# Fused attention and gated FFN: output weights loaded ahead of later pairs, wider weight rows, one value product later, a fifth E buffer

## The chip, the cores and the metric

The kernel runs on one core of a Trainium2 chip. The metric is the device time of one execution in microseconds (us); 3 to 12 executions of each kernel were taken, and medians are given.

## The reference, cut to what matters

```python
# attention: batch 8, 12 heads, 448 tokens, head size 64
scores = scale * q @ k.T;  attn = softmax(scores);  x = attn @ v      # -> 3584 tokens x 768
# FFN, width 1536
g = x @ w_gate;  val = x @ w_val
out = (g * sigmoid(g) * val) @ w_out                                  # float32
```

All inputs are float32; the kernel's DMAs cast them to float16 as they load.

## The kernel before

Two heads make a pair; 48 pairs are worked through in a loop. Step `pr` computes the scores and exponentials of pair `pr`, prepares a pair two or three steps ahead, takes products with v for two older pairs, and fills TensorE (PE) with FFN work of earlier tokens. PE, ScalarE (ACT), VectorE (DVE) and GpSimd (POOL) each do their instructions in the order of the program; the timelines below show it. GpSimd issues every casting load, so the order of loads is GpSimd's order of instructions. Parts that the argument touches:

```python
ep   = tc.tile_pool(name="ep", bufs=4)                      # E: exponentials of a pair
ps_a = tc.tile_pool(name="ps_a", bufs=1, space=PSUM)        # value products: one buffer
ps_f = tc.tile_pool(name="ps_f", bufs=3, space=PSUM)        # sums, transposes, FFN
WB = DF // 4                                                # gate and value weights: 4 tiles of 384 columns
def pv(p0, t, pool=None):      # value product of pairs p0, p0+1, half t: 16 matmuls
    acc = (pool or ps_a).tile(...)
    ...
def scaled(p0, t, acc):        # its eviction: VectorE multiplies by 1/sum, into the FFN's input X
    nc.vector.tensor_tensor(X[kk][...], acc[:, 0:S], R[p0][:], ALU.mult)
def prep(pr):                  # pairs 11 and up: POOL copies q, k; then a DMA transpose makes qkT
    ...
wq = {0: [("qk", 6), ("g", 0), ("v", 0)],
      1: [("V", 2), ("qk", 8), ("g", 1), ("v", 1)],
      3: [("g", 2), ("v", 2)],
      4: [("qk", 10), ("g", 3), ("v", 3)],
      5: [("V", 3)], 6: [("o", 0)], 7: [("o", 1)], 8: [("o", 2)]}      # loads by step
for pr in range(END):
    if not odd and 12 <= pr + LA < NPAIR:      # LA = 6
        load_qk16(pr + LA)                     # q and k of pairs pr+6, pr+7
    ... qk_half(pr, 0) ... prep(pr + 3) ...
    # even pr below 6: the sums of pairs pr-2, pr-1, copied and inverted (4 reciprocals) by VectorE
    # odd pr: scaled(pr - 3, 0, pv(pr - 3, 0)), loads of wq[pr], FFN work, qk_half(pr, 1)
    if work:
        scaled(pr - 3, 1, pv(pr - 3, 1))       # second half of the value product
```

Each third of the output weight (`wo`, 768 KB as float16) is one load. The first output product needs all three. FFN block 0 starts in step 6, once the attention of its tokens is done.

The softmax here doesn't subtract the row's maximum and nothing guards it: scores larger than these inputs give would overflow.

## Time and profile before

| | before |
|---|---|
| time, first rounds | 470.74 us median (469.92 to 472.1) |
| profiled span | 469.6 us |
| PE idle before 30.5, 67.2 to 72.0, after 464 | 4.9, 4.8, 4.4 us |
| first FFN matmul | 30.5 us |
| third 2 of the output weight lands / PE wants it | 72.0 / 67.2 us |
| PE clock halved | 70.2 to 77.0 us |

The page's chain of work that ended last, by engine, and its row of granted PE clock in 40 slices of 11.7 us (tenths of full speed):

```profile
PE 83%; DMA 13%; POOL 2%; issue 1%; ACT 0%; DVE 0%; ACTq 0%; POOLq 0%
PEclk9999997999999999999999999999999999999999
```

13% of the chain is DMA, yet 4.8 us is all that PE waits for a load: the chain was followed back from that one wait through the queue of loads to the start. Read it as "the end hangs on the queue until 72 us, and on PE after". The seventh slice has the slow clock.

### The profile page before, as it was taken

What the parts mean: (1) busy time and instruction counts of PE and PEld (TensorE: products, weight loads), DVE (VectorE), ACT (ScalarE), POOL (GpSimd) and SP (SyncE); (2) the same over time, 40 slices, a digit from 0 to 9 for tenths busy, and PEclk for the clock granted to TensorE, in tenths of its full rate; (3) what the DMA queues carried; (4) which work ended last, traced back from release to release, by engine and by line L of the source; (5) the groups of instructions that cost most, each with busy time, mean ns of one, the idle gap of its engine ahead of it and who ended that gap; (6) DMA issues with size and microseconds to landing.
All of it is one profiled execution on the core that took longest, in us unless ns stands there. A gap on an engine that the chain in (4) does not pass through costs nothing.

```text
span 469.6 us, 14109 instructions
## 1 busy us (share of the span) xinstructions
PE 455.5 (97%) x6357; PEld 228.0 (49%) x6357; DVE 237.8 (51%) x372; ACT 241.0 (51%) x348; POOL 105.3 (22%) x166
## 2 busy tenths in 40 slices
PE   7899978999999999999999999999999999999996
PEld 2344433444445555444445555444445556544453
DVE  2665662367764554546546535555456456334310
ACT  5986643765656546555446655455545552222221
POOL 8655624330450040310331131210200000000000
PEclk9999997999999999999999999999999999999999
DMA  9999999995864392944919566813423111100123
GB/s 135 195 201 200 203 170 201 151 151 60 109 93 68 36 130 60 144 77 39 140 23 126 95 96 104 116 29 75 73 33 54 36 36 35 36 6 30 35 67 101
DMA packets 80380, 44.23 MB, mean 94 GB/s; under 512 B 36672, under 2 KB 76864, under 8 KB 80320
## 3 DMA queue, kind: packets, MB, share of 16 engines
q0 software_dynamic: 40864, 23.37, 37.1%
q1 hardware_dynamic: 39392, 19.92, 23.9%
q8 instruction: 49, 0.80, 0.7%
q14 instruction: 11, 0.09, 0.1%
q10 hardware_dynamic: 64, 0.05, 0.0%
HBM read 47.19 MB, written 11.01 MB: 124 GB/s over the span
## 4 chain that ended last, share of the span: by engine, by line
PE 83%; DMA 13%; POOL 2%; issue 1%; ACT 0%; DVE 0%; ACTq 0%; POOLq 0%
PE gp L248 14%; PE op L245 13%; PE vp L248 12%; PE op L248 10%; PE vp L245 9%; PE s L182 8%; PE acc L196 7%; PE gp L245 6%; DMA wv<-in_moe_w_val_dram 5%; DMA wo<-in_moe_w_out_dram 5%; PE acc L218 3%; DMA wg<-in_moe_w_gate_dram 2%; DMA vt<-in_v_dram 1%; POOL k L118 0%; POOL q L118 0%
## 5 line engine op out<-in xcount | busy, mean ns | idle before, releaser
L189 ACT ACTIVATE E<-s 112x896 f16<-112x896 f32 x192 | 164.5, 916 | 29.1 <-PE s L182 29.1
L264 ACT ACTIVATE sg<-gp 128x384 f32<-128x384 f32 (+1 forms) x96 | 52.3, 544 | 85.8 <-PE gp L248 54.8
L276 DVE SCALAR_TENSOR_TENSOR t<-sg,gp 128x384 f32<-128x384 f32 (+1 forms) x96 | 58.6, 610 | 64.3 <-ACT sg L264 64.2
L307 ACT ACTIVATE osb<-op 128x384 f32<-128x384 f32 x55 | 27.0, 490 | 106.7 <-PE op L245 62.4
L248 PE MATMUL gp<-X,wg 128*32 128x512 f16 (+1 forms) x1416 | 78.1, 355 | 0.0
L245 PE MATMUL op<-wo,hts 128*128 128x384 f16 x396 | 69.9, 330 | 4.8 <-DMA wo<-in_moe_w_out_dram 4.8
L233 DVE RECIPROCAL R<-ssb 128x112 f32<-128x112 f32 x92 | 72.9, 827 | 0.7
L279 DVE SCALAR_TENSOR_TENSOR hts<-t,vp 128x384 f16<-128x384 f32 (+1 forms) x96 | 59.6, 621 | 22.9 <-PE vp L248 7.9
L248 PE MATMUL vp<-X,wv 128*32 128x512 f16 (+1 forms) x1224 | 66.9, 353 | 0.0
L210 DVE TENSOR_TENSOR X<-acc,R 128x448 f16<-128x448 f32 x48 | 29.9, 624 | 72.5 <-PE acc L196 70.9
L182 PE MATMUL s<-qkT 64*128 64x448 f16 x384 | 55.1, 357 | 3.6 <-ACT E L189 3.1
L245 PE MATMUL vp<-X,wv 128*128 128x384 f16 (+1 forms) x270 | 58.5, 353 | 0.0
L245 PEld LDWEIGHTS <-hts 128*128 128x128 f16 x396 | 38.4, 99 | 34.8 <-issue 9.2
L248 PEld LDWEIGHTS <-wg 128*32 128x32 f16 x1416 | 37.9, 97 | 29.5
L248 PE MATMUL op<-wo,hts 128*32 128x384 f16 x1104 | 48.9, 326 | 0.0
L127 POOL DMA_DIRECT2D vt<-in_v_dram x17 | 13.1, 768 | 155.6 <-PE acc L196 154.0
L245 PE MATMUL gp<-X,wg 128*128 128x384 f16 (+1 forms) x222 | 47.4, 350 | 0.0
L196 PE MATMUL acc<-E,vt 112*32 112x448 f16 x768 | 45.7, 360 | 0.1
L248 PEld LDWEIGHTS <-wv 128*32 128x32 f16 x1224 | 32.8, 97 | 25.4
L245 PEld LDWEIGHTS <-wv 128*128 128x128 f16 x270 | 25.3, 98 | 26.9 <-issue 4.8
L248 PEld LDWEIGHTS <-hts 128*32 128x32 f16 x1104 | 29.6, 97 | 16.3
L152 POOL COPY qk<-q 112x512 f16<-112x512 f16 x37 | 22.9, 619 | 56.2 <-DMA qkT<-qk 46.9
(37 smaller groups left out, 201.9 us busy)
## 6 DMA issues: line engine op xcount, KB each, us to landing
vt<-in_v_dram POOLq DMA_DIRECT2D x15, 336.0 KB, 5.0
q<-in_q_dram POOLq DMA_DIRECT2D x22, 224.0 KB, 5.8
k<-in_k_dram POOLq DMA_DIRECT2D x22, 224.0 KB, 7.1
out_dram<-osb SPq DMA_DIRECT2D x7, 336.0 KB, 3.1
wg<-in_moe_w_gate_dram POOLq DMA_DIRECT2D x8, 288.0 KB, 11.1
wv<-in_moe_w_val_dram POOLq DMA_DIRECT2D x8, 288.0 KB, 11.2
wo<-in_moe_w_out_dram POOLq DMA_DIRECT2D x3, 768.0 KB, 17.2
out_dram<-osb SPq DMA_DIRECT2D x8, 288.0 KB, 3.0
```

What stands on the lines that cost most here:

```text
L152: eng.tensor_copy(qk16[:, 1 - t].rearrange("p c h d -> p h c d"), src)
L182: nc.tensor.matmul(s[:, hx, 0:S], lhsT=t[ts(hx, 64)].rearrange("p c q -> p (c q)")[:, c * P : c * P + 128], rhs=t[ts(hx, 64), NC:, :].rear ...
L189: nc.scalar.activation(E[pr][:, c], s[0:P, :, 0:S], AF.Exp, scale=sm_scale)
L196: nc.tensor.matmul(acc[ts(j, 32), 0:S], lhsT=v16[g][:, 2 * r + j % 2, c, :].rearrange("p (d t) -> p t d", t=2)[:, t], rhs=E[p0 + j // 2][: ...
L210: nc.vector.tensor_tensor(X[kk][:, hp + t, ts(bb, S)], acc[:, 0:S], R[p0][:], ALU.mult)
L233: lambda i=i: nc.vector.reciprocal(rt[:, ts(i, P)], ssb[:, ts(i, P)]) for i in range(4)
L245: nc.tensor.matmul(dst, lhsT=lhsT, rhs=rhs, start=start, stop=stop)
L248: nc.tensor.matmul(dst[ts(j, 32), :], lhsT=lhsT[:, ts(j, 32)], rhs=rhs, start=start, stop=stop)
L264: nc.scalar.activation(sg[:, 0:n], gp[:, 0:n], AF.Tanh, scale=0.5)
L276: nc.vector.scalar_tensor_tensor(t1[:, 0:n], sg[:, 0:n], 1.0, gp[:, 0:n], ALU.add, ALU.mult)
L279: nc.vector.scalar_tensor_tensor(hts[:, fb, 0:n], t1[:, 0:n], 0.5 * HS, vp[:, 0:n], ALU.mult, ALU.mult)
L307: nc.scalar.activation(osb[:, ts(oh, OH)], op[:, 0:OH], AF.Copy, scale=1.0 / HS)
```

## The change

Intent: get the output weight in before PE wants it. (1) The last third goes ahead of q and k of pairs 14 and 15. (2) The last two quarters of the gate and value columns become one tile, so read rows are 3072 instead of 1536 bytes and there are four loads fewer; loads before them change places. (3) The second value product of pairs 0 and 1 moves from step 3 to step 4, which makes pair 0's E live longer, hence (4) five E buffers. (5) Both value products of step 6 go to the three-buffer pool.

```diff
-    ep = ... bufs=4
+    ep = ... bufs=5
-    WB = DF // 4                                   # four tiles of 384 columns
+    WSPL = [(0, 384), (384, 384), (768, 768)]      # three tiles
 wq:
-            1: [("V", 2), ("qk", 8), ("g", 1), ("v", 1)],
-            3: [("g", 2), ("v", 2)],
-            4: [("qk", 10), ("g", 3), ("v", 3)],
-            5: [("V", 3)],
-            6: [("o", 0)],
-            7: [("o", 1)],
-            8: [("o", 2)],
+            1: [("qk", 8), ("g", 1), ("v", 1)],
+            3: [("qk", 10), ("V", 2), ("g", 2), ("v", 2)],
+            4: [("qk", 12)],
+            6: [("V", 3), ("o", 0)],
+            7: [("o", 1), ("o", 2)],
-            if not odd and 12 <= pr + LA < NPAIR:
+            if not odd and 14 <= pr + LA < NPAIR:
-                halves = [pv(pr - 2, 0), pv(pr - 2, 1, ps_f)]
+                halves = [pv(pr - 2, t, ps_f) for t in range(2)]
-            if work:
+            if pr == 4:
+                scaled(0, 1, pv(0, 1))
+            if work and pr != 3:
                 scaled(pr - 3, 1, pv(pr - 3, 1))
```

More of the change, by code (lines that the diff above doesn't have):

```diff
@@ L70 @@
     attp = ctx.enter_context(tc.tile_pool(name="attp", bufs=4))
-    ep = ctx.enter_context(tc.tile_pool(name="ep", bufs=4))
+    ep = ctx.enter_context(tc.tile_pool(name="ep", bufs=5))
     xp = ctx.enter_context(tc.tile_pool(name="xp", bufs=2))
@@ L81 @@
     ident = consts.tile([P, P], FP16, name="ident")
-    WB = DF // 4
+    WSPL = [(0, 384), (384, 384), (768, 768)]
     wgv = {}
     for kind in "gv":
-        for i in range(4):
-            wgv[kind, i] = consts.tile([128, NCB, WB], FP16, name=f"w{kind}{i}")
+        for i, (m0, m) in enumerate(WSPL):
+            wgv[kind, i] = consts.tile([128, NCB, m], FP16, name=f"w{kind}{i}")
     def wslice(kind, fb, cb):
-        i, off = divmod(fb * 128, WB)
-        return wgv[kind, i][:, cb, ds(off, 128)]
+        i = min(fb // 3, 2)
+        return wgv[kind, i][:, cb, ds(fb * 128 - WSPL[i][0], 128)]
     wo = [consts.tile([128, NFB // 3, DM], FP16, name=f"wo{i}") for i in range(3)]
@@ L137, in load_w @@
         else:
-            src = (moe_w_gate if kind == "g" else moe_w_val)[:, ts(i, WB)].rearrange(
+            src = (moe_w_gate if kind == "g" else moe_w_val)[:, ds(*WSPL[i])].rearrange(
                 "(a p t) m -> t p a m", p=128, t=2
```

## The prediction

> **What bounds the kernel now.** I read the page first: TensorE (PE) is busy 97% of a 469.6 us span, so only its 14 idle us and any slow clock can be won without removing work, and the change removes none. The cut into stretches tells where those us are. Its columns are PE, weight load, VectorE, ScalarE and GpSimd busy us (instructions), granted PE clock, DMA share, GB/s.
>
> ```profile
> 0.00:30.50 30.50, 25.61 (x337) 11.10 (x337) 16.68 (x29) 23.33 (x28) 20.85 (x34) 1.00 1.21 173
> 30.50:67.20 36.70, 36.70 (x322) 18.19 (x321) 23.69 (x41) 24.37 (x35) 16.78 (x25) 1.00 1.32 192
> 67.20:72.00 4.80, 0.00 (x1) 0.00 (x0) 0.00 (x0) 0.00 (x0) 3.11 (x5) 0.81 1.21 193
> 72.00:80.00 8.00, 8.00 (x58) 2.84 (x58) 0.68 (x2) 3.64 (x6) 3.15 (x5) 0.69 1.40 188
> 80.00:464.00 384.00, 384.00 (x5638) 195.37 (x5637) 196.35 (x301) 189.31 (x280) 61.36 (x99) 1.00 0.49 76
> ```
>
> The 14 idle us are 4.9 before 30.5 (start-up, and PE waiting for exponentials), 4.8 in the third row and 4.4 after 464 (the last output leaving). From 80 to 464 us PE never idles and its clock is full: nothing to win there, but any us won or lost earlier carries to the end whole. From 67.2 to 72.0 PE does nothing at all, and until 80 it is busy at a clock of 0.69. The list of waits names the reason, PE's timeline the place:
>
> ```profile
> PE op L245 <- DMA wo<-in_moe_w_out_dram: 4.8, 1, 4.8
> ```
>
> ```profile
> 65.74 1.46 PE L245 MATMUL op<-wo,hts 128*128 128x384 f16 x8
> 72.00 1.44 PE L245 MATMUL op<-wo,hts 128*128 128x384 f16 x4 [4.80 <-DMA wo<-in_moe_w_out_dram]
> 73.37 0.93 PE L182 MATMUL s<-qkT 64*128 64x448 f16 x4
> ```
>
> The first output product of block 0 does eight matmuls with thirds 0 and 1 of the output weight, then waits for third 2. GpSimd's timeline shows when each third was issued:
>
> ```profile
> 44.13 0.75 POOL L144 DMA_DIRECT2D wo<-in_moe_w_out_dram  x1 [0.47 <-DMA k<-in_k_dram]
> 45.65 0.74 POOL L144 DMA_DIRECT2D wo<-in_moe_w_out_dram  x1 [0.77 <-DMA wg<-in_moe_w_gate_dram]
> 47.94 0.72 POOL L118 DMA_DIRECT2D q<-in_q_dram  x1 [1.55 <-issue]
> 48.65 0.70 POOL L118 DMA_DIRECT2D k<-in_k_dram  x1
> ...
> 50.46 0.75 POOL L144 DMA_DIRECT2D wo<-in_moe_w_out_dram  x1
> ```
>
> The q and k of pairs 14 and 15 stand ahead of third 2. The three thirds took 13.9, 17.2 and 21.5 us to land, so they landed at 58.1, 62.8 and 72.0. The queue has been full since 12 us, at about 200 GB/s: order in it decides.
>
> **What the Trainium skill says.** "TensorE: Matmul & The Clock Gate", section What's actually happening: the PE clock halves after an idle window of about 3.4 us and comes back after a similar busy one. The trace agrees roughly: its clock records halve it at 70.2, 3.0 us into the wait, and restore it at 77.0, 5.0 us after work resumed. "Perfetto Trace Analysis", section Roofline: a single core is bounded by its 16 DMA engines, about 435 GB/s. These loads read fp32 and write fp16, so 200 GB/s written is 400 read: near it, and more transfers in flight will not help. "DMA: Bandwidth & Descriptors", section Why small descriptors are slow: some 3 cycles of 32 bytes per packet. Read rows of 1536 bytes are 48 beats, of 3072 bytes 96, so doubling the row saves 51/48 against 99/96, an estimate of 3%. The trace: a stretch nearly all narrow weight rows (20 to 24 us) ran at 202 GB/s, one of wide output rows with transposes (56 to 60 us) at 203.
>
> **The change part by part.**
> 1. Third 2 ahead of pairs 14 and 15. Removed ahead of it: 2 x 224 KB = 0.46 MB. In the kernel before, 0.46 + 0.79 MB landed in 72.0 - 62.8 = 9.2 us, or 136 GB/s (the DMA transposes of q and k, used from pair 11 on, share the engines there, and the packet records of the trace show every queue standing still from 63.5 to 64.8). At that rate 0.46 MB is 3.4 us: landing at 68.6. Alternatively third 1's own 4.7 us after third 0 gives 67.5, plus the standstill of 1.3 us: 68.8.
> 2. Wider rows: 4 x 590 KB = 2.36 MB, 11.8 us at 200 GB/s; 3% is 0.35 us earlier for all behind. Landing then about 68.3.
> 3. All else up to third 2 (q, k up to pair 13, V0 to V3, gate and value) is reordered, not added. The wide value columns land about where the last narrow ones did (49.7, or 49.4); block 0 now needs them at its seventh column block, 48.6 on PE's timeline before, not the tenth. A wait of up to 0.8 us is possible here.
> 4. The moved value product. It has 16 matmuls, 0.87 us, wherever it stands; nothing is removed. But it writes the one buffer of its pool, and VectorE's order decides when that comes free. Before:
>
> ```profile
> 20.54 0.62 DVE L210 TENSOR_TENSOR X<-acc,R 128x448 f16<-128x448 f32 x1 [0.47 <-PE acc L196]
> 21.90 0.62 DVE L230 COPY ssb<-acc 128x448 f32<-128x448 f32 x1 [0.74 <-PE acc L218]
> 22.56 2.99 DVE L233 RECIPROCAL R<-ssb 128x112 f32<-128x112 f32 x4
> 25.46 0.56 DVE L171 COPY qkT<-tp 128x896 f16<-128x896 f16 x1
> 25.94 0.61 DVE L210 TENSOR_TENSOR X<-acc,R 128x448 f16<-128x448 f32 x1
> ```
>
> ```profile
> 24.58 0.94 PE L196 MATMUL acc<-E,vt 112*32 112x448 f16 x16
> ```
>
> Before, the product was evicted at 20.54 by an idle VectorE. After (the built order shows it), its eviction stands behind the sum copy, four reciprocals and a transpose copy. The sums end some 0.5 us sooner (21.4), so the eviction ends at 21.4 + 0.62 + 2.99 + 0.56 + 0.61 = 26.2. The next product (pairs 2 and 3, first half; 24.58 before) needs that buffer. PE would come to it at about 24.1 and wait 2.1 us. How I get 24.1: until then ScalarE sets the pace (its timeline has 12 exponentials in 10.03 us, 0.84 each, and the scores have two buffers, so PE runs two ahead). Its idle gap of 0.69 at 20.2, which the product caused before, goes; pair 4's four exponentials then end at 23.5; the scores of pair 5 follow once PE has done the transposes of pair 6 and the moved product, at 24.1. Behind it to the first gate matmul: 0.87 + 0.5 + 0.6 + 0.87 + 0.9 + 1.63 + 0.5 = 5.9, so 32.1 instead of 30.5: **1.6 us later**. In exchange ScalarE loses one idle gap of 0.7 us, which does not reach the end.
> 5. The fifth E buffer is what lets pair 4 start while the moved product still needs pair 0's E; PE is in order and full later, so by itself nothing. Two halves of pair 4 in the three-buffer pool: avoids one more wait on the single buffer.
>
> Sum: PE would need third 2 at 67.2 + 1.6 = 68.8 and it lands at about 68.3. So the wait goes (-4.8), the slow clock goes ((77.0 - 72.0)/2 = -2.5), the start costs +1.6, and I allow +0.4 for leftover waits: 471.4 - 5.3 = 466.1.
>
> **The rivals.** (a) VectorE does not hold PE up (tracking finer than I read): then PE needs third 2 at 67.2, waits about 1.1 us, below what lowers the clock: 471.4 - 7.3 + 1.1 + 0.4 = 465.6. Almost the same time, as the landing sets it; the chosen path and this one differ only in which wait is seen. (b) DMA takes the win back: wide weight packets crowd the transpose of pair 11, which landed at 63.0 against a need at 63.4; now everything beside it is wide. Or third 2 lands at 70 or later because the transposes take their share. Then 1 to 3 us of waiting: 467 to 469. At 3 us the clock may halve again: 470. Against: PE's need also moves 1.6 us later, and the transposes' work is the same. (c) Wide rows really speed the queue by 10% or more and PE never waits: 471.4 - 7.3 = 464.1 if the start costs nothing too. Against: equal GB/s in stretches of narrow and wide rows. (d) ScalarE becomes the bound: no, it is idle half of the span after 30 us.
>
> **Range and chances.** Between full win (464.1) and win mostly given back (469) lies my 8-in-10 range, 463.8 to 468.8; the runs before spread by 2 us. Faster by 2% is below 462.0: more than the whole 7.3 + 0.4 us at hand, so 0.03. Slower by 2% needs a new loss of 17 us: 0.01.
>
> **What would show it.** Right: in the profile after, the wait on the output weight is below 1 us, the PE clock is full throughout, a new PE wait of about 2 us on VectorE's eviction near 24 to 26 us, the first gate matmul near 32.1, third 2 landing near 68, PE full from there to the end. Wrong: a first gate matmul at 30.5 (step 4 false); a PE wait on a qkT transpose or on the wide value weights; a halved clock anywhere; new idle PE after 80 us, which I have ruled out.

## The result, and the profile after

The changed kernel took 465.56 us median (465.34 to 465.79, 4 runs) against 470.74 (4 runs). The ratio is 0.9887, 95% interval 0.9859 to 0.9915: 1.1% less, and 0.5 us from the forecast. (A ratio here is the mean time of one kernel's fast runs over that of the other's in the same rounds, so not quite the ratio of the medians.)

The same chain and clock rows, after:

```profile
PE 94%; ACT 2%; DMA 1%; DVE 1%; POOL 1%; issue 0%; POOLq 0%
PEclk9999999999999999999999999999999999999999
```

DMA has left the chain and no slice is slow. The stretches, with the same columns as in the prediction:

```profile
0.00:32.20 32.20, 25.14 (x337) 11.12 (x337) 16.59 (x29) 23.27 (x28) 21.74 (x36) 1.00 1.21 176
32.20:67.40 35.20, 35.20 (x314) 17.42 (x313) 23.07 (x40) 24.54 (x35) 12.21 (x18) 1.00 1.26 198
67.40:72.00 4.60, 4.60 (x42) 2.25 (x40) 1.42 (x3) 2.10 (x3) 1.72 (x3) 1.00 1.36 182
72.00:80.00 8.00, 8.00 (x74) 3.56 (x72) 3.61 (x5) 5.27 (x8) 5.29 (x9) 1.00 1.62 161
80.00:458.00 378.00, 378.00 (x5595) 192.30 (x5588) 192.79 (x296) 185.19 (x275) 61.13 (x98) 1.00 0.48 76
```

The third row is the stretch in which PE did nothing before; now it is full, at full clock. The first row is 1.7 us longer: the FFN starts at 32.2 instead of 30.5. (Some 0.5 us of that arise before the moved product: here PE waited 0.3 us for a load of k near 9.9 us, and the exponentials of pair 1 began at 10.63 instead of 10.17.) The list of PE's waits (total, times, longest) has no load of weight in it any more, and a new second line:

```profile
PE s L182 <- ACT E L189: 2.8, 6, 0.8
PE acc L196 <- DVE X L210: 2.1, 1, 2.1
```

PE's timeline shows where that wait is, and that the first output product now does its twelve matmuls in one go; VectorE's shows what PE waited for:

```profile
26.70 0.94 PE L196 MATMUL acc<-E,vt 112*32 112x448 f16 x16 [2.14 <-DVE X L210]
32.20 1.15 PE L245 MATMUL gp<-X,wg 128*128 128x384 f16 x6
67.42 2.11 PE L245 MATMUL op<-wo,hts 128*128 128x384 f16 x12
```

```profile
22.00 0.62 DVE L230 COPY ssb<-acc 128x448 f32<-128x448 f32 x1 [1.48 <-PE acc L218]
22.66 2.99 DVE L233 RECIPROCAL R<-ssb 128x112 f32<-128x112 f32 x4
25.57 0.56 DVE L171 COPY qkT<-tp 128x896 f16<-128x896 f16 x1
26.04 0.61 DVE L210 TENSOR_TENSOR X<-acc,R 128x448 f16<-128x448 f32 x1
```

The eviction of the moved product ends at 26.65, and the next product starts at 26.70. GpSimd's timeline has the new order of the loads:

```profile
41.10 0.74 POOL L144 DMA_DIRECT2D wo<-in_moe_w_out_dram  x1 [1.51 <-DMA wg<-in_moe_w_gate_dram]
43.90 0.74 POOL L144 DMA_DIRECT2D wo<-in_moe_w_out_dram  x1 [2.05 <-DMA wg<-in_moe_w_gate_dram]
46.67 0.71 POOL L118 DMA_DIRECT2D q<-in_q_dram  x1 [2.04 <-DMA wv<-in_moe_w_val_dram]
49.48 0.70 POOL L118 DMA_DIRECT2D k<-in_k_dram  x1 [2.09 <-DMA wv<-in_moe_w_val_dram]
```

Third 2 took 23.2 us to land, the longest of the three, so it landed at 43.9 + 23.2 = 67.1. PE wants it after eight matmuls of 0.163 us, at 67.42 + 1.30 = 68.7: there are 1.6 us to spare.

### The profile page after: what moved, and what is told of

Same layout as the page of the kernel before. It is cut to its first block, busy times and chain, and to the rows that moved or that the text cites. A ratio compares the mean times of both kernels' runs of the same rounds, so it can differ in the third digit from the quotient of the medians.

```text
span 464.0 us, 14105 instructions
## 1 busy us (share of the span) xinstructions
PE 452.6 (98%) x6357; PEld 227.4 (49%) x6357; DVE 237.8 (51%) x372; ACT 241.0 (52%) x348; POOL 102.1 (22%) x162
## 4 chain that ended last, share of the span: by engine, by line
PE 94%; ACT 2%; DMA 1%; DVE 1%; POOL 1%; issue 0%; POOLq 0%
PE gp L248 15%; PE op L245 14%; PE vp L248 13%; PE vp L245 11%; PE op L248 10%; PE gp L245 9%; PE s L182 9%; PE acc L196 9%; PE acc L218 4%; ACT E L189 2%; DMA k<-in_k_dram 1%; DVE R L233 1%; PE tp L166 1%; POOL q L118 0%; POOL k L118 0%
## 5 line engine op out<-in xcount | busy, mean ns | idle before, releaser
L245 PE MATMUL op<-wo,hts 128*128 128x384 f16 x396 | 68.5, 327 | 0.0
L210 DVE TENSOR_TENSOR X<-acc,R 128x448 f16<-128x448 f32 x48 | 29.9, 624 | 66.3 <-PE acc L196 64.7
```

The source lines that it names most:

```text
L210: nc.vector.tensor_tensor(X[kk][:, hp + t, ts(bb, S)], acc[:, 0:S], R[p0][:], ALU.mult)
L245: nc.tensor.matmul(dst, lhsT=lhsT, rhs=rhs, start=start, stop=stop)
```

## The experiments

Theory: the order of the loads is the win (third 2 in time, and with it the clock), and the moved product costs 1.6 us of start. Rivals: the wide rows are the win; the place of the product is a gain or a matter of indifference. All kernels below gave correct results. "Full clock" lists the runs at 0.997 and up. Runs 1 to 4, 5 to 8 and 9 to 12 shared a chip and the runs of the kernel before each: medians 471.52, 471.21 and 470.69 us.

| run | edit | median us | ratio to before | full-clock runs |
|---|---|---|---|---|
| e1 | before, third 2 first | 467.25 | 0.9911 | 465.89, 466.10, 466.44 |
| e2 | after, pairs 14, 15 first | 470.53 | 0.9986 | none |
| e3 | after, narrow rows | 467.18 | 0.9916 | 466.10, 467.28 |
| e4 | after, product back | 465.16 | 0.9867 | 464.62 to 465.31 (3) |
| e5 | before, product late | 468.80 | 0.9964 | none |
| e6 | after, product in the other pool | 466.56 | 0.9913 | 466.24 to 466.73 (4) |
| e7 | after, 1.3 us more matmuls | 468.95 | 0.9959 | 466.87 |
| e8 | before, 1.3 us more matmuls | 469.96 | 0.9991 | 468.90, 468.88 |
| e9 | after | 466.48 | 0.9904 | 465.36 to 465.87 (3) |
| e10 | as e3 | 465.97 | 0.9902 | 465.25 to 466.00 (4) |
| e11 | as e4 | 465.94 | 0.9885 | 465.45 to 466.04 (3) |
| e12 | e11, pair 11 early | 467.74 | 0.9927 | 465.62 to 467.29 (3) |

### The order: e1 alone, e2 undone

e1, kernel before:

```diff
-            7: [("o", 1)],
-            8: [("o", 2)],
+            7: [("o", 1), ("o", 2)],
```

> The kernel before with one edit: third 2 of the output weight is issued ahead of q and k of pairs 14 and 15. Order theory: nearly the whole win, and a little more than the whole change, as the start is not delayed: first gate matmul at 30.5 us, third 2 lands at 67 to 68.5 against a need at 67.2, PE clock full, 464.3 us (463.5 to 465.5). Rival, wide rows bring the win: third 2 still lands late, the wait stays over 2 us, 468 us or more.

e2, changed kernel, the same two lines the other way round.

> The changed kernel with only this undone: q and k of pairs 14 and 15 go ahead of third 2 again. Order theory: third 2 lands 3 to 4 us later than in the changed kernel (67.1), near 70.5; PE needs it at 68.7 and waits about 2 us, the clock may stay full: 467.5 us (466.5 to 470). Rival, wide rows or the product's place bring the win: within 0.5 us of the changed kernel's 465.6.

e2 gave all of the win back: 470.53, more than the 466.5 to 470 expected. Its PE timeline has the old wait again, and its clock was halved from 72.6 to 79.5:

```profile
73.96 1.44 PE L245 MATMUL op<-wo,hts 128*128 128x384 f16 x4 [5.35 <-DMA wo<-in_moe_w_out_dram]
```

Third 2 landed at 73.9 instead of 67.1, 6.8 us later. The same swap in the kernel before (e1) moved it by 4.5, from 72.0 to 67.4; I had charged 3.4 for these loads of 0.46 MB. Part of the 6.8 is no matter of what stands right ahead of third 2: the profiled run of e2 was the slowest of its six (473.68), and in it thirds 0 and 1 landed 1.6 and 1.7 us later than in the profile after already (59.4 and 63.7). The transposes of pair 11 were issued earlier there (49.0 instead of 51.4), which takes engine time from the thirds. The packet records show how transposes and loads share the engines: the DMA transposes, whose packets are 256 bytes, moved 27 to 31 GB/s while the loads beside them wrote rows of 1536 bytes (the output weight), and mostly 57 to 64 GB/s beside written q and k rows of 512 bytes. This is not the main part: from the landing of third 1 to that of third 2 the loads as a whole moved 131 GB/s before and 127 after.

e1 took nearly all of the win (0.9911) with two lines. It missed its 464.3, for a reason that the rival path of the prediction had named. Third 2 landed at 67.4 and was waited for no more (the first output product does its twelve matmuls in one go); pair 11 was waited for instead:

```profile
67.96 2.11 PE L245 MATMUL op<-wo,hts 128*128 128x384 f16 x12
```

```profile
PE s L182 <- DMA qkT<-qk: 1.7, 1, 1.7
```

The transpose of pair 11 landed at 65.6, and PE wanted it at 63.9. So the order is the win, with or without the wide rows, and one load taken out of the way uncovers the next. What is left between e1's full-clock runs and the first runs of the changed kernel, 0.6 us (means of 466.1 and 465.6, perhaps on different chips), belongs to the other edits together; the new places of the other loads and part (5) were not tried alone.

### The rows: e3 and e10

Changed kernel, narrow tiles again, same places:

```diff
-    WSPL = [(0, 384), (384, 384), (768, 768)]
+    WSPL = [(0, 384), (384, 384), (768, 384), (1152, 384)]
-        i = min(fb // 3, 2)
+        i = fb // 3
-            3: [("qk", 10), ("V", 2), ("g", 2), ("v", 2)],
+            3: [("qk", 10), ("V", 2), ("g", 2), ("g", 3), ("v", 2), ("v", 3)],
```

> The changed kernel with the gate and value columns in four narrow tiles again, all else kept. Order theory: third 2 lands within 0.5 us of 67.1, which is under the need at 68.7, so the time is the same: 465.6 us, within 0.5. Rival, wide rows speed the queue by 10%: the weights take 1 us more, third 2 lands at 68.2 or later, and the first late value block waits; 466 us or more.

> Narrow gate and value rows in the changed kernel once more, on the same chip as it. If the 1.6 us that it seemed to cost was the chip or the early halving of the PE clock in its profile: within 0.5 us of the changed kernel here. If wide rows are worth it: 1 us or more over it, in runs whose clock is full too.

e3 came out 1.6 us over the changed kernel of the first rounds, against my expectation; but the chip of those rounds is not on record, and e3's profiled run had its clock halved early. (Of its two full-clock runs one, 467.28, stays unexplained.) e10 and e9 on one chip settle it: full-clock runs 465.25 to 466.00 with narrow rows, 465.36 to 465.87 with wide ones. Third 2 landed at 67.6 with narrow rows in e10 (issue at 47.7 and 19.9 us) and at 67.1 in the profile after: the rows are worth about 0.5 us of landing (single profiles; e3's has 68.0), all of it inside the 1.6 us to spare. The rival falls.

### The place of the product: e4, e11, e6

e4 and e11 are the same kernel, the changed one with the product back in step 3:

```diff
-            if pr == 4:
-                scaled(0, 1, pv(0, 1))
-            if work and pr != 3:
+            if work:
                 scaled(pr - 3, 1, pv(pr - 3, 1))
```

> The changed kernel with the value product of pairs 0 and 1 back at its old place (five E buffers kept). Theory that the moved product costs: the 2.1 us wait on the eviction goes, the first gate matmul comes 1.2 us earlier (near 31.0), third 2 is needed at 67.5 and lands at 67.1: 464.4 us (463.8 to 465.3). Rival, the landing sets the end whatever the start does: 465.6 us, within 0.3, with a new wait of 1.2 us on third 2. Rival, the move helps: slower than 466.

> The value product back at its old place in the changed kernel once more. 0.6 us under the changed kernel if the earlier start is mostly eaten by a wait on the DMA transpose of pair 11 (seen in the run of the order alone: 1.7 us); 1.2 under if nothing eats it. In a profile with a full clock from the start: first gate matmul near 31, and a PE wait on that transpose of 1 to 1.7 us.

e4 was 0.4 us under the first result, whose chip is not on record. On one chip, e11's full-clock runs (465.45 to 466.04) lie on those of e9 (465.36 to 465.87): no gain. PE's timeline of e11 tells why:

```profile
30.47 1.15 PE L245 MATMUL gp<-X,wg 128*128 128x384 f16 x6
...
49.42 0.99 PE L245 MATMUL vp<-X,wv 128*128 128x384 f16 x5 [0.57 <-DMA wv<-in_moe_w_val_dram]
...
65.21 0.55 PE L182 MATMUL s<-qkT 64*128 64x448 f16 x4 [1.05 <-DMA qkT<-qk]
...
67.55 2.11 PE L245 MATMUL op<-wo,hts 128*128 128x384 f16 x12
```

The FFN does start 1.73 us earlier than after (30.47 against 32.20). Then PE waits 0.57 us for the wide value weight and 1.05 us for pair 11, 1.62 in all, and the first output product starts at 67.55 against 67.42. So the late product's cost (1.2 to 1.5 us of these 1.73, see below) is real where it arises and worth nothing at the end: whoever starts earlier waits longer for the queue.

e6 keeps the product late but takes the cause of its wait away:

```diff
-                scaled(0, 1, pv(0, 1))
+                scaled(0, 1, pv(0, 1, ps_f))
```

> The changed kernel with the moved product in the three-buffer pool instead of the single buffer. If the single buffer, held until VectorE has done the reciprocals, is what makes PE wait: the 2.1 us wait shrinks to 0.6 or less, the first gate matmul comes about 1 us earlier, 464.6 us (464.0 to 465.3). If PE waits for something else there: no change, 465.6.

The 2.1 us wait vanished from the list of waits, which shows that the single buffer caused it. The time did not fall: all six runs lie between 466.24 and 466.73, on a chip on which the unedited changed kernel was not run. (An estimate for that chip: e7's full-clock run, 466.87, less its 1.3 us of added work is 465.6, so e6 was rather about 0.9 slower than faster.) Its profiled run had the clock halved from 13.7 to 20.5 us and started the FFN at 32.9, so what its full-clock runs waited for was not seen. That stays open.

### What the wait absorbs: e5, e8, e7

e5 is the kernel before with only the late product and the fifth E buffer; e7 and e8 add six matmuls on a constant tile:

```diff
+            if pr == FIRST + 1:
+                dummy(6)
```

> The kernel before with only the value product moved and the fifth E buffer. The start is delayed by 1.2 to 1.6 us, but the wait on third 2 (4.8 us) absorbs it: the wait shrinks to about 3.4, and the time stays that of the kernel before within 0.5 us (470.2 to 471.2), unless the shorter wait spares part of the slow clock (then 469). If the delay is not absorbed: 472 or more. If the move itself were a gain: below 468.5.

> The kernel before with the same six extra matmuls. The wait on third 2 absorbs them: its wait shrinks from 4.8 to 3.5 us, and the time stays within 0.5 us of the kernel before, 470.7. If PE time alone sets the end: 472.0.

> The changed kernel with six extra matmuls on the warm-up tile (1.3 us of PE) just after the first FFN stretch. Nothing absorbs them if third 2 is in time: 465.6 + 1.3 = 466.9 us. If some wait still sets the time: less, 465.6.

A later start made the kernel before faster: e5 by 2.4 us of median (468.80 against 471.21; ratio 0.9964, interval 0.9939 to 0.999), e8 only in three of its six runs, by 2.3 (468.9); as a whole e8 is level with the kernel before (0.9991, interval 0.996 to 1.0022). The lists of waits of their profiles, e5 first:

```profile
PE op L245 <- DMA wo<-in_moe_w_out_dram: 1.4, 1, 1.4
```

```profile
PE op L245 <- DMA wo<-in_moe_w_out_dram: 2.8, 1, 2.8
```

Third 2 landed at 71.6 and 71.7, as before; PE just came later. The wait of 4.8 us had halved the clock; after these two it stayed full, by the clock records (e5 had a halving of 3.4 us earlier, at 26.2, which only made PE later still). That accounts for the 2.5 us. I had expected the time to stay and named the clock only for e5. Of the three runs of e8 at 468.9 two were at full clock and one at 0.993; the three others took 471.0 to 472.1 at 0.993 to 0.996 and have no profile. e7 shows the other side: with the queue out of the way nothing absorbs 1.3 us, and its only full-clock run took 466.87, 1.3 over 465.56. Its five others took 468.25 to 469.69 at 0.993 to 0.996.

### Unedited once more: e9, and the early halving

> The changed kernel, unedited, on the chip of the next three: what they are compared with. 465.6 us, within 0.7.

Six runs: three at full clock, 465.36 to 465.87, and three at 0.990 to 0.994, 467.1 to 468.4; their median, 466.48, is just outside the range expected. The profiled one was of the latter. Two of its stretches:

```profile
12.00:18.00 6.00, 5.21 (x60) 2.06 (x60) 2.41 (x4) 4.86 (x7) 3.63 (x5) 0.72 1.42 193
24.00:30.00 6.00, 3.86 (x52) 1.33 (x46) 4.22 (x7) 2.82 (x5) 3.41 (x5) 0.79 1.36 201
```

The clock was halved twice for 3.4 us before the FFN, once from 13.8 and once from 27.5 us, the second time within PE's wait of 2.14 us on the moved product's eviction (it ended at 27.77). The first FFN matmul came at 34.67, 2.47 us later than in the profile after, and the span was 466.6 against 464.0, 2.6 longer: what is lost early carries to the end whole when the load is in time. The kernel before seems to have such runs too (468.0 to 468.3 at 0.990 and 0.991), but there a late start shortens the wait, as in e5. The last section tells what seems to decide in which runs the clock is halved.

### A try at more: e12

e11, with the copies and the transpose of pair 11 ahead of the loads of pairs 14 and 15:

```diff
-            if not odd and 14 <= pr + LA < NPAIR:
+            if not odd and 16 <= pr + LA < NPAIR:
                 load_qk16(pr + LA)
             ... prep(pr + 3)
+            if pr == 8:
+                load_qk16(14)
```

> The same, and GpSimd copies and transposes pair 11 before it issues q and k of pairs 14 and 15. The transpose of pair 11 lands near 56 instead of 64 us, so PE no longer waits for it; third 2 shares the engines longer and lands near 68, PE needs it at about 67.3. If the wait on pair 11 ate the gain: 464.0 to 464.8 us, below the run before. If the bytes in the queue are what holds: a wait of up to 1 us on third 2 takes its place, and the time is that of the run before, 465.0.

The transpose of pair 11 landed at 57.3 and was waited for no more. In its place:

```profile
PE op L245 <- DMA wo<-in_moe_w_out_dram: 2.4, 1, 2.4
PE vp L245 <- DMA wv<-in_moe_w_val_dram: 0.5, 1, 0.5
```

Third 2 landed at 70.3 instead of 67.1, and the median is 467.74: both expectations missed. By the packet records the transposes had moved 0.19 MB more by 54 us than in e11, and the loads 0.24 MB less: moved ahead, the transposes push the weight back. The profile is of a run of 469.04; two others took 465.62 and 465.96, no longer than e11, so in them third 2 can hardly have been so late. Of all the versions run none is clearly better than the changed kernel; the product's old place (e4, e11) is as good, and its eight runs, one at 0.993 on each chip among them, stayed within 464.6 to 466.1, with none of the 467 to 468 that e9 and e10 have. That the late product's wait can bring on a halving is shown by two profiles (at 26.2 in e5, at 27.5 in e9; none of the six with the product in its old place has one there). How much more frequent it makes the slower runs is not settled by so few.

## Why the prediction was right

**The bound and the two terms of the win** were right. The wait of 4.8 us went, the clock stayed full (2.5 us), and from 80 us on PE is full in both profiles. e1 and e2 show the order to be the cause; e5, and e8 where its clock stayed full, show the clock term by itself.

**Landing of third 2: 68.3 predicted, 67.1 measured.** Right in kind, mis-sized in two terms. Third 1 landed 0.9 us earlier than before already (62.0 instead of 62.8), where the rows were to bring 0.35. Third 2 then followed after 5.1 us, where 9.2 - 3.4 = 5.8 had been reckoned, so the loads taken out of its way were worth 4.0 us there and not 3.4 (3.8 in e1 against before). The rate is not what failed: 136 GB/s reckoned, 131 by the packets. Why it was more than 3.4 stays open. PE's need, 68.8 predicted, was 68.7.

**Wide rows: 0.35 us predicted, about 0.5 measured**, and no time, as e10 shows. (The narrow stretch that the prediction gives as 202 GB/s reads 201.)

**The value weight's wait, up to 0.8 us "possible":** absent after, where the start is late; 0.57 and 0.5 us in e11 and e12, where it is early.

**The moved product: 2.1 us of wait and 1.6 of later start predicted; 2.14 and 1.2 to 1.5 measured** (e6 shows the buffer to be the reason). The 1.73 between e11 and after hold more than the product: pair 1's exponentials began at 10.37 in e11 and at 10.63 after, which leaves 1.5; in e1 they began at 10.63 too, and its FFN at 30.98, which leaves 1.2. PE came to the buffer at 24.56 and the eviction ended at 26.65, both 0.5 us after the forecast 24.1 and 26.2, as late as what precedes them; the rest up to the first gate matmul took 5.5 us and not 5.9. That the forecast 32.1 met 32.2 was luck: the late load of k made up for the 0.4. And its "+1.6" in the sum was no cost of the change. Without it PE waits 1.62 us for loads. Rival (a) said so, almost the same time since the landing sets it, but expected the wait on third 2; it came on the value weight and on pair 11's transpose, the one that rival (b) had feared.

**The allowance of 0.4 us for leftover waits:** the profile after has none on a load. The sum came within 0.5 us all the same, -5.3 predicted and -5.2 measured. In part that is luck: landing, start and allowance erred in ways that the 1.6 us to spare hides.

**Not foreseen:** the early halving of the clock in some runs, which costs the changed kernel 1.5 to 2.8 us (e9), while in the kernel before the wait takes part of it up. The full-clock runs are what 465.6 describes.

## What to carry to other kernels

When a full queue feeds an engine that is full after it, order the queue by when each transfer is wanted, and expect the next load in line to become the wait: judge a start that is earlier or later against the landing times behind it, since up to that point only the queue counts. A wait that halves the PE clock costs its own length and then some (4.8 and 2.5 us here); shortening it, even by making work arrive later, can win the second part. Compare runs by their granted clock before explaining a difference of one or two microseconds.

## What the Trainium skill lacked or had wrong

- "TensorE: Matmul & The Clock Gate", What's actually happening: an idle window of about 3.4 us halves the clock, a busy one restores it, and the windows of 3413 ns run freely. Agreed here: within each profile every change of the clock lies on one grid of 3.41 us (the records last 3.41, 6.83, 10.24 us and so on), and the window counts, not the length of the wait. Waits of 4.8 (before), 5.4 (e2) and 2.4 us (e12) halved the clock; one of 2.8 us (e8) fell across two windows and did not. The windows of before, of e12 and the two of e8, with PE's busy us after the comma:

```profile
66.79:70.20 3.41, 0.41 (x3) 0.12 (x2) 0.00 (x0) 0.00 (x0) 2.27 (x4) 1.00 1.18 198
67.62:71.03 3.41, 0.97 (x6) 0.30 (x4) 0.00 (x0) 0.00 (x0) 0.00 (x0) 1.00 1.47 145
66.64:70.05 3.41, 2.23 (x14) 1.23 (x13) 1.54 (x3) 0.64 (x1) 2.43 (x4) 1.00 1.21 197
70.05:73.47 3.42, 1.76 (x20) 0.74 (x23) 0.00 (x0) 0.91 (x2) 0.69 (x2) 1.00 1.30 185
```

In e12 the clock fell at 71.0, when PE had been at work again since 70.3. The 5.0 us that the kernel before took to regain full clock hold one whole busy window (73.6 to 77.0), so they agree as well. Lacking: how busy is busy enough. In the 14 profiles, up to 86 us, the clock fell after every window at full clock with PE busy up to 46% (e9's second fall, 1.57 of 3.41 us), after none with 63% or more, after four at 58 to 62%, all of them early (e9's first fall: 2.01 of 3.41 us, up to 13.8), and not after five at 50 to 58% (e1: 1.72 of 3.42 us, up to 66.3). So it seems to hang on where the grid falls on PE's idle times which runs lose clock early.
- No page that I found has it: while DMA transposes and loads were both in flight, all queues stood nearly still, or slowed, for about 1.3 us. The two stretches of the kernel before show it (the last column is GB/s): 28 against 186 (97 in the like stretch after). In each profile it came about a microsecond after an instruction fetch of 16 KB had begun (62.4 and 63.5 before, 63.6 and 64.4 after). That fetch comes 31.3 to 33.4 us after the first FFN matmul in the profiles of all twelve experiments and both kernels, so it moves with PE. That the fetch is its cause is not shown.

```profile
63.50:64.80 1.30, 1.30 (x21) 0.40 (x19) 1.18 (x2) 1.30 (x3) 0.00 (x0) 1.00 0.88 28
64.80:66.00 1.20, 1.20 (x12) 0.75 (x9) 1.09 (x2) 0.80 (x1) 0.37 (x1) 1.00 1.34 186
```

- "DMA: Bandwidth & Descriptors", Why small descriptors are slow: its 3 cycles per packet gave an estimate of 3% for doubled rows; that is 0.35 us of these loads' 11.8, and the runs show about 0.5, which does not contradict it. The same page, Queues, rings and completion order, says that engines alternate between queues by packets but not what that does to transposes beside wide rows: 27 to 31 GB/s beside written rows of 1536 bytes, mostly 57 to 64 beside rows of 512.
